# Decay attention into a softplus FFN on one core: three attention units loaded ahead of the weights, the weights' top bits shared between ScalarE and VectorE, and 12 instead of 10 units with whole float32 operands

## The chip, the cores and the metric

The kernel runs on one core of a Trainium2 chip. The metric is the device time of one execution in microseconds (us). Before the change it was 701.85 us, the median of three runs from 699.92 to 701.89.

## What is computed

A linear attention with a decay per head feeds a two-layer FFN with a softplus between the layers. Inputs q, k, v are float32 of shape (4, 8, 768, 64); the weights are float64 of shape (512, 2048) and (2048, 512).

```python
gamma = 1.0 - 2.0 ** (-5.0 - np.arange(H, dtype=np.float32))
for t in range(S):
    state = gamma[None, :, None, None] * state + np.einsum('bhd,bhe->bhde', k[:, :, t], v[:, :, t])
    y[:, :, t] = scale * np.einsum('bhd,bhde->bhe', q[:, :, t], state)
...
x = np.ascontiguousarray(attn_out.transpose(0, 2, 1, 3)).reshape(B * S, H * D)
h = x @ w_in
g = np.maximum(h, 0.0) + np.log1p(np.exp(-np.abs(h)))
return (g @ w_out).astype(np.float32)
```

## The kernel before

**Attention.** The sequence is cut into chunks of C = 128 tokens. A unit is one chunk of one batch entry for half of the heads (4 heads): 48 units, in the order batch, chunk, half. Within a unit the work is quadratic, and a state of 64 x 64 per head carries the decay over to the next chunk. A unit goes through these parts:

- `load_unit` (L104): three loads on SP's queue, kn, qn, vn, of 128 KB each, with three buffers of each.
- `decay` (L113): GpSimd multiplies qn and vn by the decay tables.
- `operands` (L120): TensorE transposes kn and qn into the PSUM tile tp; ScalarE and VectorE copy it out.
- `scores` (L156): TensorE makes sc = k q^T, ScalarE copies it to ah, GpSimd masks it (L177).
- `new_state` (L182): TensorE makes pp = k^T v; VectorE adds it to the running sum td. The last chunk of a sequence leaves this out.
- `stack_and_outputs` (L259): ScalarE copies the state to st; TensorE makes yp from st and qw and from vn and ah; ScalarE casts it to xh (L255), VectorE writes the remainder xl (L257).

Tiles tp, sc, pp and yp share three PSUM buffers.

**Precision.** A product of two float32 operands is made in one of two ways. For the first WHOLE = 10 units the operands stay float32 ("whole"): one matmul, which the trace shows as two rows. For later units each operand is split into a high part in float32r and a remainder, and a product is made of three float32r matmuls or of matmuls with the parts side by side (L139 to L153, L171, L195, L242 to L251). The split needs more copies and subtractions on ScalarE and VectorE.

**Weights.** The float64 weights are loaded as 16 slices f of both matrices (`load_weights`, L62; 512 KB each, on SP's queue) and converted in place of a cast (`convert_weights`, L74). For each slice of w_in and of w_out, words low and high are the two halves of a float64. ScalarE rescales the high word (L82) and takes the top three bits of the low word into wp by a multiplication with a rounding offset (L87). VectorE joins sign and bits (L88, L89) into the float32 w. ScalarE casts w to its float32r high part (L91), GpSimd subtracts for the remainder (L92). wp is one buffer in PSUM; w has two. The load of slice f waits for the casts of slice f - FETCH (3).

**FFN.** For blocks of T = 256 tokens and pairs of slices, `hidden` (L279) makes 24 matmuls into hp (L286 to L288), softplus runs over VectorE, ScalarE, VectorE, ScalarE, GpSimd (L293 to L302), and `second` (L305), two steps later, adds 12 matmuls into acc (L316 to L318).

**Order.** Parts of unit u are due at tick 4u plus an offset (`PARTS`, L264). A first loop (L371) runs the ticks up to those of block 0; in it, every fourth tick loads one slice of weights and, from the fourth slice on, converts one. Then the steps follow, with ticks planned between them. The program is then ordered on each engine by a scheduler with a timeline of its own, so that the order of a queue isn't that of the code: it is read from the compiled order. Each engine works its list in order.

Of the kernel before, what the change touches and what calls it, by code (L numbers as in the profile page):

```python
# [14 lines left out]
AF = mybir.ActivationFunctionType  # L15
ALU = mybir.AluOpType
# [3 lines left out]
T = 256  # L20
AHEAD = 2
EARLY = 2
WHOLE = 10
TURN = 5
LAG = 2
FETCH = 3
SLACK = 2.0**-17
# [3 lines left out]
def decay_attention_then_softplus_ffn(ctx: ExitStack, tc: tile.TileContext, q, k, v, w_in, w_out, qtab, vtab, gtab, out):  # L31
    nc = tc.nc
# [27 lines left out]
    raw, win, wout, converts = {}, {}, {}, {}  # L60

    def load_weights(f):  # L62
        fs = slice(f * P, (f + 1) * P)
        raw[f] = [const.tile([P, ND * P], I64, name=nm, tag=f"{nm}{f}") for nm in ("win", "wout")]
        loads_of_f = (
            nc.sync.dma_start(raw[f][0].rearrange("p (c w) -> p c w", c=ND), w_in[:, fs].rearrange("(c p) w -> p c w", p=P)),
            nc.sync.dma_start(raw[f][1], w_out[fs, :]),
        )

        if f >= FETCH:  # L70
            for load, after in zip(loads_of_f, converts[f - FETCH]):
                tc.add_manual_dep(load.ins, after.name, mybir.DependencyInfo(mybir.DependencyClass.Sync, mybir.DependencyReason.SCHED_ONLY), reason="pace")

    def convert_weights(f):  # L74

        n = ND * P
        converts[f] = []
        for nm, bits, to in zip(("win", "wout"), raw.pop(f), (win, wout)):
            words = bits.bitcast(U32).rearrange("p (n t) -> p n t", t=2)
            low, high = words[:, :, 0], words[:, :, 1]  # L80

            nc.scalar.activation(high.bitcast(F32), high.bitcast(F32), AF.Copy, scale=2.0**-112)  # L82

            wp = ps_w.tile([P, n], U32, name="wp")
            w = wts.tile([P, n], U32, name="w")

            nc.scalar.activation(wp, low, AF.Copy, scale=(1 - SLACK) * 2.0**-29, bias=7.5 * SLACK - 0.5)  # L87
            nc.vector.scalar_tensor_tensor(wp, high, 0x80000000, wp, op0=ALU.bitwise_and, op1=ALU.bitwise_or)  # L88
            nc.vector.scalar_tensor_tensor(w, high, 3, wp, op0=ALU.logical_shift_left, op1=ALU.bitwise_or)  # L89
            to[f] = const.tile([P, 2, n], F32R, name=f"{nm}hl", tag=f"{nm}{f}")  # L90
            converts[f].append(nc.scalar.copy(to[f][:, 0], w.bitcast(F32)).ins)  # L91
            nc.gpsimd.tensor_tensor(to[f][:, 1], w.bitcast(F32), to[f][:, 0].bitcast(F32), op=ALU.subtract)  # L92
# [3 lines left out]
    loads, live, state, xs = {}, {}, {}, {}  # L96
# [5 lines left out]
    qws = [attn.tile([P, 2, NJ, C], F32, name="qw", tag="vhl", bufs=2) for i in range(2)]  # L102

    def load_unit(n):  # L104
        b, c, hf = units[n]
        tiles = []
        for nm, src in (("kn", k), ("qn", q), ("vn", v)):
            t = attn.tile([P, HH, D], F32, name=nm, bufs=3)
            nc.sync.dma_start(t, src[b, hf * HH:(hf + 1) * HH, c * C:(c + 1) * C, :].rearrange("h s d -> s h d"))
            tiles.append(t)  # L110
        loads[n] = tiles
# [8 lines left out]
    def operands(n):  # L120
# [5 lines left out]
        for j in range(NJ):  # L126
            nc.tensor.transpose(tp[:, 1, j, :], qn[:, 2 * j:2 * j + 2, :], ident)  # L127
        if n < WHOLE:
            kw = attn.tile([P, NJ, C], F32, name="kw", tag="kh")
# [26 lines left out]
    def scores(n):  # L156
        kq = live[n][0]
        if n < WHOLE:
            kw, qw = kq
# [22 lines left out]
    def new_state(n):  # L182
# [4 lines left out]
        pp = ps_a.tile([D, HH, 2, D], F32, name="pp", tag="a")  # L187
        if n < WHOLE:
            kn, vn = live[n][1:3]
# [10 lines left out]
        else:  # L200
            td = state[hf][1]
            nc.vector.tensor_tensor(td, pp[:, :, 0, :], td, op=ALU.add)
        if n >= WHOLE:
            nc.vector.tensor_tensor(td, pp[:, :, 1, :], td, op=ALU.add)
        state[hf] = [None, td]

    def stack_state(n):
# [3 lines left out]
        tdv = state[hf][1].rearrange("d (j p) e -> d p j e", p=2)  # L211
        if n + 2 < WHOLE:
            st = attn.tile([P, NJ, D], F32, name=f"st{hf}", bufs=2)
# [13 lines left out]
    def outputs(n):  # L227
# [7 lines left out]
        for j in range(NJ):  # L235
            for par in range(2):
                h = 2 * j + par
                o = yp[:, par, j, :]
                if c and n < WHOLE:
                    nc.tensor.matmul(o, lhsT=st[:, j, :], rhs=kq[1][:, par, j, :], start=True, stop=False)  # L240
# [21 lines left out]


    PARTS = {-6: load_unit, -2: decay, 0: operands, 2: scores, 3: new_state, 5: stack_and_outputs}  # L264
    FIRST_TICK = min(PARTS)
    PERIOD = 4
# [3 lines left out]
    def tick(n):  # L270
        for at, part in PARTS.items():
            u, r = divmod(n - at, PERIOD)
            if r == 0 and 0 <= u < len(units):
                part(u)
# [64 lines left out]
    def ticks_for(i):  # L339

        return min(per_block * (i + 1) + max(PARTS) - PERIOD + 1 + AHEAD, last_tick + 1)

    done, loaded, converted = FIRST_TICK + 1, 0, 0

    def convert_to(n):
        nonlocal loaded, converted
        while converted < min(NF, n):
            convert_weights(converted)
            converted += 1
            if loaded < NF:  # L350
                load_weights(loaded)
                loaded += 1

    tick(FIRST_TICK)

    nc.scalar.dma_start(qtabs[:, 0], qtab)
    nc.scalar.dma_start(vtabs[:, 0], vtab)
# [13 lines left out]
    while done < ticks_for(0):  # L371
        tick(done)
        done += 1
        if done % 4 == 2:
            if loaded >= FETCH:
                convert_weights(converted)
                converted += 1
            load_weights(loaded)
            loaded += 1
# [66 lines left out]
```

## Time and profile before

| | |
|---|---|
| median of three runs | 701.85 us (699.92, 701.85, 701.89) |
| the profiled execution | 700.03 us |
| its span, first to last instruction | 698.2 us |
| ScalarE, VectorE, GpSimd busy | 372.1, 433.2, 281.4 us |
| DMA | 42.82 MB |

The profile is of one execution, whose own time is 700.03 us. PE is TensorE's matmuls, PEld its weight loads, DVE VectorE, ACT ScalarE, POOL GpSimd, SP the queue that issues the loads. L286 is line 286 of the kernel before. In a row of the timeline the first number is the start in us from the span's begin, the second the duration; a bracket names the idle time ahead and what ended it. In a row of a group stand the busy time of all, the mean of one in ns, and the idle time ahead. Starts of neighbouring matmuls are closer than their durations, since matmuls are pipelined: what one costs in a dense stretch is the distance of two starts.

### The profile page before, as it was taken

What the parts mean: (1) busy time and instruction counts of PE and PEld (TensorE: products, weight loads), DVE (VectorE), ACT (ScalarE), POOL (GpSimd) and SP (SyncE); (2) the same over time, 40 slices, a digit from 0 to 9 for tenths busy, and PEclk for the clock granted to TensorE, in tenths of its full rate; (3) what the DMA queues carried; (4) which work ended last, traced back from release to release, by engine and by line L of the source; (5) the groups of instructions that cost most, each with busy time, mean ns of one, the idle gap of its engine ahead of it and who ended that gap; (6) DMA issues with size and microseconds to landing.
All of it is one profiled execution on the core that took longest, in us unless ns stands there. A gap on an engine that the chain in (4) does not pass through costs nothing.

```text
span 698.2 us, 13537 instructions
## 1 busy us (share of the span) xinstructions
PE 684.4 (98%) x5056; PEld 621.3 (89%) x5056; DVE 433.2 (62%) x893; ACT 372.1 (53%) x835; POOL 281.4 (40%) x324
## 2 busy tenths in 40 slices
PE   6899999999999999999999999999999999999997
PEld 4688889899999999999999999999999999999996
DVE  4676785557666766557667666647766676544221
ACT  6988885446556546445555555445555544543221
POOL 5676667334343342343334333433433333222221
PEclk9999999999999999999999999999999999999999
DMA  9976650122112112111111111211211110000000
GB/s 266 287 201 173 192 159 1 31 61 69 31 23 69 31 25 61 31 31 54 39 23 37 49 38 24 61 37 25 62 24 39 54 31 16 31 1 1 31 1 30
DMA packets 90752, 42.82 MB, mean 61 GB/s; under 512 B 77376, under 2 KB 85568, under 8 KB 90688
## 3 DMA queue, kind: packets, MB, share of 16 engines
q1 hardware_dynamic: 90240, 41.96, 22.2%
q8 instruction: 40, 0.66, 0.4%
q14 instruction: 24, 0.20, 0.1%
q10 hardware_dynamic: 448, 0.01, 0.0%
HBM read 35.66 MB, written 6.29 MB: 60 GB/s over the span
## 4 chain that ended last, share of the span: by engine, by line
PE 96%; ACT 1%; issue 0%; DVE 0%; ACTq 0%
PE hp L286 14%; PE hp L287 13%; PE hp L288 13%; PE acc L316 13%; PE acc L317 13%; PE acc L318 13%; PE sc L171 3%; PE tp L125 1%; PE tp L127 1%; PE pp L195 1%; PE yp L250 1%; PE yp L251 1%; PE yp L249 1%; PE yp L246 1%; PE yp L240 1%; PE yp L243 1%
## 5 line engine op out<-in xcount | busy, mean ns | idle before, releaser
L286 PE MATMUL hp<-xh,winhl 128*128 128x256 f32 x768 | 221.4, 289 | 0.4 <-ACT xh L255 0.4
L288 PE MATMUL hp<-xh,winhl 128*128 128x256 f32 x768 | 217.9, 284 | 0.0
L287 PE MATMUL hp<-xl,winhl 128*128 128x256 f32 x768 | 217.6, 283 | 0.0
L302 POOL TENSOR_TENSOR gl<-sp,gh 128x512 fp32r<-128x512 f32 x96 | 125.4, 1306 | 149.3 <-ACT gh L300 86.7
L316 PE MATMUL acc<-wouthl,gh 128*128 128x512 f32 x384 | 154.3, 402 | 0.0
L317 PE MATMUL acc<-wouthl,gh 128*128 128x512 f32 x384 | 150.4, 392 | 0.0
L318 PE MATMUL acc<-wouthl,gl 128*128 128x512 f32 x384 | 149.1, 390 | 0.0
L286 PEld LDWEIGHTS hp<-xh,winhl 128*128 128x128 f32 x768 | 146.5, 191 | 2.8 <-issue 0.5
L287 PEld LDWEIGHTS hp<-xl,winhl 128*128 128x128 f32 x768 | 147.0, 191 | 1.6 <-issue 0.5
L288 PEld LDWEIGHTS hp<-xh,winhl 128*128 128x128 f32 x768 | 146.8, 191 | 0.6 <-issue 0.3
L293 DVE TENSOR_SCALAR sp<-hp 128x512 uint32<-128x512 uint32 x96 | 66.1, 690 | 70.6 <-PE hp L288 61.0
L300 ACT CAST gh<-sp 128x512 fp32r<-128x512 f32 x96 | 59.5, 620 | 74.1 <-PE acc L317 57.4
L117 POOL TENSOR_TENSOR qn<-qn,qtabs 128x256 f32<-128x256 f32 x48 | 29.4, 613 | 151.1 <-DMA qn<-in_q_dram 125.0
L294 ACT ACTIVATE sp<-sp 128x512 f32<-128x512 f32 x96 | 60.9, 634 | 49.0 <-DVE sp L293 48.7
L318 PEld LDWEIGHTS acc<-wouthl,gl 128*128 128x128 f32 x384 | 71.9, 188 | 15.6
L316 PEld LDWEIGHTS acc<-wouthl,gh 128*128 128x128 f32 x384 | 72.4, 189 | 12.5 <-issue 0.5
L317 PEld LDWEIGHTS acc<-wouthl,gh 128*128 128x128 f32 x384 | 72.5, 189 | 11.4
L298 DVE SCALAR_TENSOR_TENSOR sp<-hp,sp 128x512 f32<-128x512 f32 x96 | 65.9, 687 | 12.8 <-ACT sp L294 11.6
L142 DVE TENSOR_TENSOR kq<-tp,kq 64x256 fp32r<-64x256 f32 x76 | 32.1, 422 | 67.0 <-ACT kq L140 65.8
L139 ACT CAST kq<-tp 64x512 fp32r<-64x512 f32 x76 | 44.1, 581 | 40.0 <-PE tp L127 38.8
L255 ACT CAST xh<-yp 64x256 fp32r<-64x256 f32 x96 | 35.1, 366 | 51.0 <-PE yp L251 44.5
L257 DVE TENSOR_TENSOR xl<-yp,xh 64x256 fp32r<-64x256 f32 x96 | 39.9, 416 | 33.7 <-ACT xh L255 32.7
(85 smaller groups left out, 1082.6 us busy)
## 6 DMA issues: line engine op xcount, KB each, us to landing
win<-in_moe_w_in_dram SPq DMA_DIRECT2D x16, 512.0 KB, 4.5
wout<-in_moe_w_out_dram SPq DMA_DIRECT2D x16, 512.0 KB, 4.4
kn<-in_k_dram SPq DMA_DIRECT2D x48, 128.0 KB, 2.3
qn<-in_q_dram SPq DMA_DIRECT2D x48, 128.0 KB, 2.8
vn<-in_v_dram SPq DMA_DIRECT2D x48, 128.0 KB, 2.2
out_dram<-o SPq DMA_DIRECT2D x24, 256.0 KB, 2.1
gtab_sb<-in_gtab_dram ACTq DMA_DIRECT2D x2, 2.0 KB, 3.8
qtabs<-in_qtab_dram ACTq DMA_DIRECT2D x1, 4.0 KB, 2.4
```

The source lines that it names most:

```text
L139: nc.scalar.copy(kq[own, :2, par], tp[own])
L286: nc.tensor.matmul(hp[:, k], lhsT=wt[:, 0, d, :], rhs=xh[:, d, :], start=d == 0, stop=False)
L287: nc.tensor.matmul(hp[:, k], lhsT=wt[:, 0, d, :], rhs=xl[:, d, :], start=False, stop=False)
L288: nc.tensor.matmul(hp[:, k], lhsT=wt[:, 1, d, :], rhs=xh[:, d, :], start=False, stop=d == ND - 1)
L293: nc.vector.tensor_scalar(sp.bitcast(U32), hps[s].bitcast(U32), 0x80000000, None, op0=ALU.bitwise_or)
L294: nc.scalar.activation(sp, sp, AF.Softplus)
L298: nc.vector.scalar_tensor_tensor(g, hps.pop(s), 0.0, g, op0=ALU.max, op1=ALU.add)
L300: nc.scalar.copy(gh, g)
L302: nc.gpsimd.tensor_tensor(gl, sps.pop(s), gh.bitcast(F32), op=ALU.subtract)
L316: nc.tensor.matmul(acc[i][t], lhsT=gh[:, k, ts], rhs=wt[:, 0], start=begins and k == 0, stop=False)
L317: nc.tensor.matmul(acc[i][t], lhsT=gh[:, k, ts], rhs=wt[:, 1], start=False, stop=False)
L318: nc.tensor.matmul(acc[i][t], lhsT=gl[:, k, ts], rhs=wt[:, 0], start=False, stop=ends and k == 1)
```

## The change

Three edits.

1. Loads: units 0, 1 and 2 are loaded ahead of the first weights; `load_unit` returns at once for a unit that is loaded. The first loop starts one tick earlier; weights are loaded at its first tick and then at every fourth, one tick later than before, so that after it as many slices are loaded (6) and converted (3) as before.
2. Top bits: ScalarE takes them for w_out as before; for w_in VectorE shifts the low word right by 29 bits.
3. WHOLE is 12: units 10 and 11, the last chunk of batch entry 0, have whole float32 operands.

```diff
-WHOLE = 10
+WHOLE = 12
...
-            nc.scalar.activation(wp, low, AF.Copy, scale=(1 - SLACK) * 2.0**-29, bias=7.5 * SLACK - 0.5)
+            if nm == "wout":
+                nc.scalar.activation(wp, low, AF.Copy, scale=(1 - SLACK) * 2.0**-29, bias=7.5 * SLACK - 0.5)
+            else:
+                nc.vector.tensor_scalar(wp, low, 29, None, op0=ALU.logical_shift_right)
...
     def load_unit(n):
+        if n in loads:
+            return
...
-    done, loaded, converted = FIRST_TICK + 1, 0, 0
+    done, loaded, converted = FIRST_TICK, 0, 0
...
-    tick(FIRST_TICK)
+
+    for n in range(3):
+        load_unit(n)
...
-        if done % 4 == 2:
+        if done % 4 == 3 and done > 0 or done < 0 and loaded == 0:
```

Line numbers after are higher by 5 behind the edits: L82 stays, L87 is L88, L91 is L94, L131 is L136, L164 is L169, L255 is L260, L286 is L291.

On SP's queue the first 15 loads were kn, qn, vn and a slice of win and wout for units 0, 1 and 2 in turn; now the nine loads of the three units come first, then two slices of win and wout, then kn and qn of unit 3.

ScalarE's list from its first instruction on data, kw of unit 0, before (kw, qw: copies of the transposed operands; st: state; winhl, wouthl: the float32r weights):

```order
L131 COPY kw<-tp 128x256
L132 COPY qw<-tp 64x256
L82 ACTIVATE win<-win 128x512
L87 ACTIVATE wp<-win 128x512
L82 ACTIVATE wout<-wout 128x512
L214 COPY st_178<-td_167 64x128
L215 COPY st_178<-td_167 64x128
L164 COPY ah<-sc 128x512
L91 CAST winhl<-w 128x512
L87 ACTIVATE wp<-wout 128x512
L131 COPY kw<-tp 128x256
L132 COPY qw<-tp 64x256
```

The same place after:

```order
L136 COPY kw<-tp 128x256
L137 COPY qw<-tp 64x256
L219 COPY st_178<-td_167 64x128
L220 COPY st_178<-td_167 64x128
L169 COPY ah<-sc 128x512
L136 COPY kw<-tp 128x256
L137 COPY qw<-tp 64x256
L82 ACTIVATE win<-win 128x512
L260 CAST xh<-yp 64x2x128 x2
L82 ACTIVATE wout<-wout 128x512
L169 COPY ah<-sc 128x512
L94 CAST winhl<-w 128x512
```

The conversion of the first slice has moved behind unit 1's operands, and the first cast of weights behind unit 1's ah.

TensorE's list around the first hidden-layer matmul (hp), before; pp ahead of it is that of unit 3:

```order
L240 MATMUL yp<-qw,st_178 64x128
L246 MATMUL yp<-ah,vn 64x128
L191 MATMUL pp<-vn,kn 64x64 x4
L286 MATMUL hp<-xh,winhl 128x256 x2
L125 MATMUL tp<-ident,kn 128x128 x2
L127 MATMUL tp<-ident,qn 128x128 x2
L240 MATMUL yp<-qw,st_228 64x128
L287 MATMUL hp<-xl,winhl 128x256
```

And after:

```order
L245 MATMUL yp<-qw,st_178 64x128
L251 MATMUL yp<-ah,vn 64x128
L168 MATMUL sc<-qw,kw 128x128 x4
L291 MATMUL hp<-xh,winhl 128x256
L292 MATMUL hp<-xl,winhl 128x256
L293 MATMUL hp<-xh,winhl 128x256
L291 MATMUL hp<-xh,winhl 128x256
L292 MATMUL hp<-xl,winhl 128x256
L293 MATMUL hp<-xh,winhl 128x256
L196 MATMUL pp<-vn,kn 64x64 x4
L130 MATMUL tp<-ident,kn 128x128 x2
L132 MATMUL tp<-ident,qn 128x128 x2
```

Unit 3's sc has moved directly ahead of the first hp, and its pp behind the first six; these now include products with xl.

## The prediction

> **What bounds the kernel now.** I read the page first, then the busy time by windows, then the timeline of the first 34 us, and at last the groups by form for single prices. The page:
>
> ```profile
> span 698.2 us, 13537 instructions
> PE 684.4 (98%) x5056; PEld 621.3 (89%) x5056; DVE 433.2 (62%) x893; ACT 372.1 (53%) x835; POOL 281.4 (40%) x324
> PE 96%; ACT 1%; issue 0%; DVE 0%; ACTq 0%
> ```
>
> The third line is the chain that ended last: 96% of it is TensorE (PE). The windows tell where the rest lies (columns: length, busy us of PE, weight loads, VectorE, ScalarE, GpSimd, then clock, DMA share, GB/s):
>
> ```profile
> 0.00:10.00 10.00, 4.75 (x21) 3.65 (x22) 2.83 (x15) 4.25 (x8) 4.45 (x17) 1.00 0.84 225
> 10.00:20.00 10.00, 7.73 (x49) 5.62 (x47) 6.53 (x12) 8.89 (x21) 7.88 (x10) 1.00 1.16 316
> 20.00:30.00 10.00, 7.79 (x63) 6.21 (x62) 6.28 (x12) 8.96 (x21) 6.54 (x8) 1.00 1.10 296
> 30.00:40.00 10.00, 10.00 (x83) 8.86 (x82) 7.55 (x15) 9.15 (x21) 6.99 (x9) 1.00 0.79 222
> 80.00:90.00 10.00, 10.00 (x74) 8.81 (x74) 8.09 (x13) 8.80 (x18) 7.45 (x8) 1.00 0.59 167
> 90.00:100.00 10.00, 10.00 (x68) 8.97 (x67) 8.74 (x15) 8.24 (x16) 5.25 (x5) 1.00 0.47 131
> ```
>
> From 30 us on PE has no idle time. So the change can act in two ways only: it can start the dense stretch earlier, in the first 28 us, or it can change the amount of PE work behind that. In those 28 us the busy engine is ScalarE (8.89 and 8.96 of 10 us). The rows that mark the start (start us, duration, engine, line):
>
> ```profile
> 3.60 0.66 PE L125 MATMUL tp<-ident,kn 128*128 128x128 f32 x2 [3.60 <-DMA kn<-in_k_dram]
> 6.82 0.66 ACT L82 ACTIVATE win<-win 128x512 f32<-128x512 f32 x1 [0.28 <-DMA win<-in_moe_w_in_dram]
> 8.36 1.65 PE L163 MATMUL sc<-qw,kw 128*128 128x128 f32 x6
> 10.05 0.59 ACT L164 COPY ah<-sc 128x512 f32<-128x512 f32 x1 [0.26 <-PE sc L163]
> 11.40 1.64 PE L246 MATMUL yp<-ah,vn 128*64 128x128 f32 x8 [0.17 <-POOL ah L177]
> 26.90 0.74 ACT L255 CAST xh<-yp 64x256 fp32r<-64x256 f32 x2 [0.93 <-PE yp L246]
> 27.70 0.51 PE L286 MATMUL hp<-xh,winhl 128*128 128x256 f32 x2 [0.37 <-ACT xh L255]
> ```
>
> The first FFN matmul (27.70) waits for the xh cast of unit 2, which ScalarE reaches at 26.90. From there on hidden-layer matmuls fill every gap that attention leaves.
>
> **The change part by part: the start.** Prices of ScalarE's steps, means over the whole run:
>
> ```profile
> L82 ACT ACTIVATE win<-win 128x512 f32<-128x512 f32 x16 | 10.8, 678 | 2.1 <-DMA win<-in_moe_w_in_dram 2.1
> L82 ACT ACTIVATE wout<-wout 128x512 f32<-128x512 f32 x16 | 10.8, 676 | 1.5 <-DMA wout<-in_moe_w_out_dram 1.3
> L87 ACT ACTIVATE wp<-wout 128x512 uint32<-128x512 uint32 x16 | 10.1, 634 | 0.0
> L87 ACT ACTIVATE wp<-win 128x512 uint32<-128x512 uint32 x16 | 10.1, 631 | 0.0
> L91 ACT CAST wouthl<-w 128x512 fp32r<-128x512 f32 x16 | 9.9, 618 | 5.1 <-DVE w L89 5.0
> L91 ACT CAST winhl<-w 128x512 fp32r<-128x512 f32 x16 | 9.9, 616 | 1.0 <-DVE w L89 0.9
> L164 ACT COPY ah<-sc 128x512 f32<-128x512 f32 x10 | 5.8, 579 | 1.6 <-PE sc L163 1.4
> L131 ACT COPY kw<-tp 128x256 f32<-128x256 f32 x10 | 3.7, 366 | 3.8 <-PE tp L127 3.8
> L132 ACT COPY qw<-tp 64x256 f32<-64x256 f32 x10 | 3.6, 362 | 0.0
> L214 ACT COPY st<-td 64x128 f32<-64x128 f32 x8 | 2.3, 289 | 0.0
> L255 ACT CAST xh<-yp 64x256 fp32r<-64x256 f32 x96 | 35.1, 366 | 51.0 <-PE yp L251 44.5
> ```
>
> I count ScalarE's instructions in its order from the first ah copy (10.05 us) to the end of unit 2's xh pair. Before, they are 35: 3 ah, 3 pairs of kw and qw, 2 pairs of st, 3 pairs of xh, 6 of L82, 5 of L87 and 5 of L91. By the rows that is 3 x 0.58 + 3 x 0.73 + 2 x 0.58 + 3 x 0.73 + 6 x 0.68 + 5 x 0.63 + 5 x 0.62 = 17.6 us. The trace takes from 10.05 to 26.90 + 0.74 = 27.64, also 17.6 us: small waits and small overlaps cancel, so the sum is a fair clock.
>
> After, 30 instructions stand there. The 3 ah, the 3 kw/qw pairs, 2 st pairs and 3 xh pairs are the same; L82 is again 6, but the top bits on ScalarE are only 2 and the casts 3. Sum: 17.6 - 3 x 0.63 - 2 x 0.62 = 14.5 us, so 3.1 us less. Of this, the top bits of w_in are what moved to VectorE; the rest is conversions that stand later, since the weights are loaded later. The first ah can't come earlier: it waits for the six sc matmuls at 8.36, which end at 10.01, and PE's order up to there is the same.
>
> Part of the 3.1 us is lost. After the order goes ah, kw, qw, L82, and is through with these at 10.05 + 0.58 + 0.37 + 0.36 + 0.68 = 12.0. The next is unit 0's xh, which waits for the yp matmuls at 11.40 + 1.64 = 13.0. Before, other conversion steps filled that hole. So 1.0 us of waiting is new, and the first FFN matmul comes 2.1 us earlier, at about 25.6. It also has less behind it: PE's order before has unit 3's pp matmuls ahead of it, after they stand behind. Their cost is the distance of two starts, 33.68 - 33.07 = 0.6 us (rows below). What the start gains is 2.1 - 0.6 = **1.5 us**. Its ends: nothing, if ScalarE waits elsewhere as much as it saves, and 3.1 us, if the new wait and the pp cost vanish in other gaps.
>
> The three early units by themselves give little: of PE's waits in the rows above only the first, at 3.60, is for a load. The weights come later instead: six more loads of 0.13 MB stand ahead of them, 0.79 MB at 225 to 316 GB/s, about 2.9 us. The first L82 could then start at 6.82 + 2.9 = 9.7; ScalarE comes to it at 11.4. This costs nothing as long as that margin of 1.7 us holds; past it each us is paid in full by the casts behind. On SP's queue the loads of unit 3 now stand behind two sets of weights, before behind three. On GpSimd the decay of units 1 and 2 moves ahead of the first low parts of the weights, for which only the third matmul of each hidden group waits.
>
> **The half pace at the start.** The same matmuls are slow at first: six sc matmul rows take 1.65 us at 8.36, eight take 1.16 at 31.98, and pp falls from 1.12 us at 7.32 to the following:
>
> ```profile
> 7.32 1.12 PE L191 MATMUL pp<-vn,kn 128*64 128x64 f32 x8
> 14.52 0.68 PE L191 MATMUL pp<-vn,kn 128*64 128x64 f32 x8
> 30.31 0.43 PE L246 MATMUL yp<-ah,vn 128*64 128x128 f32 x2
> 31.98 1.16 PE L163 MATMUL sc<-qw,kw 128*128 128x128 f32 x8
> 33.07 0.68 PE L191 MATMUL pp<-vn,kn 128*64 128x64 f32 x8
> 33.68 0.51 PE L286 MATMUL hp<-xh,winhl 128*128 128x256 f32 x2
> ```
>
> The clock column of the windows says 1.00 all along, so it doesn't show this. I take it to end where it ended, between 11.4 and 14.5 us, since PE does the same work up to there; the sum above rests on that. The Trainium skill, "TensorE: Matmul & The Clock Gate", Part 1, has TensorE start at half clock, released by one busy window of about 3.4 us whose phase is free, and taken back by an idle one. The factor in these rows agrees with that. By that rule a start one window earlier is possible, and it would make the sum that of the faster rival below; an idle stretch of a whole window would make it worse, and my longest one is about 2 us.
>
> **Units 10 and 11 with whole operands.** This is PE work in the dense stretch and is paid in full. Rows of the split form, and two rows for the pitch of whole matmuls:
>
> ```profile
> 125.57 0.38 PE L240 MATMUL yp<-qw,st 128*64 128x128 f32 x2
> 125.79 0.38 PE L246 MATMUL yp<-ah,vn 128*64 128x128 f32 x2
> 129.51 0.64 PE L171 MATMUL sc<-kq 128*128 128x256 f32 x4
> 130.00 0.40 PE L316 MATMUL acc<-wouthl,gh 128*128 128x512 f32 x1
> 136.06 0.22 PE L242 MATMUL yp<-kq,st 128*64 128x128 f32 x1
> 137.26 0.33 PE L171 MATMUL sc<-kq 128*128 128x256 f32 x1
> ```
>
> Split: 4 sc matmuls take 130.00 - 129.51 = 0.49 us, 20 yp matmuls 137.26 - 136.06 = 1.20, together 1.69. Whole: one matmul (two rows) is 125.79 - 125.57 = 0.22, so 4 + 8 of them are 2.64, which is 0.95 more; for two units 1.9. Measured in place with the changes of shape around them, sc is 33.07 - 31.98 = 1.09 and seven yp matmuls 31.98 - 30.31 = 1.67, eight 1.91: 3.00, or 1.31 more, for two units 2.6. Both units are the last chunk of their sequence and have no pp. I take **2.1 us**, near the lower end, because PE's order after has fewer stretches of like matmuls in all (398 against 411 by my count), so the changes of shape that the two units add are saved elsewhere. What they save on ScalarE and VectorE lies beside a full PE and is worth nothing there.
>
> **Top bits of w_in on VectorE.** The nearest row is a one-source step of the same size:
>
> ```profile
> L293 DVE TENSOR_SCALAR sp<-hp 128x512 uint32<-128x512 uint32 x96 | 66.1, 690 | 70.6 <-PE hp L288 61.0
> ```
>
> 16 x 0.69 = 11.0 us more on VectorE, spread to about 105 us, and 16 x 0.63 = 10.1 us less on ScalarE. The tightest windows, 80 to 100, have 1.9 + 1.3 = 3.2 us of VectorE idle; about three of the 16 steps fall there, 2.1 us, and unit 10's splits leave. It fits: cost zero, hidden by PE; if it didn't fit, PE would wait one for one.
>
> **Sum.** The profiled execution took 700.03 us, 1.8 more than its span. 700.03 - 1.5 + 2.1 = 700.6. The three runs are 699.92, 701.85 and 701.89; the profile resembles the lowest, and the median is 1.8 higher. Put on the median the forecast is **702.4**, 0.6 above it. 0.3%, or 2.1 us, is about what a measurement of this kernel can tell from no change.
>
> **The rivals.**
>
> *The start runs at full pace (faster).* With units 1 and 2 there early, PE reaches full pace before the first sc. Then the six sc cost 0.9 instead of 1.65, pp 0.7 instead of 1.1, yp 0.95 instead of 1.64, and the new 1.0 us wait goes: 2.8 us more, with the 1.5 a gain of 4.3, so 701.85 - 4.3 + 2.1 = 699.6. For it: the slow rows. Against it: PE's early waits are for ScalarE and GpSimd, not for loads. Chance 0.2, with whatever else shortens the start.
>
> *VectorE's longer chain takes the place of the ScalarE step (slower).* ScalarE works in order; its cast of w_in waits for VectorE, which now runs three dependent steps for it, and xh and ah of the units queue behind that cast. If each of the three casts ahead of the first FFN matmul waits 0.69 us, 2.1 us are lost: 701.85 + 2.1 + 2.1 - 1.5 = 704.5. For it: the casts of wouthl waited 5.0 us for VectorE before. Against it: winhl only 0.9, and the shift needs the load alone, so it can run ahead. It decides once these waits exceed 1.5 us in sum. Chance 0.18.
>
> *The change doesn't do what it says (slower or same).* ScalarE's freed time goes into waiting, the start gains nothing, the whole units stay: 701.85 + 2.1 = 704.0, on the border of 0.3%. Chance 0.12, half to each side.
>
> **How the numbers follow.** The forecast has 0.50; its own range, with gain 0 to 3.1 and cost 1.9 to 2.6, is 700.6 to 704.5. Faster by over 0.3%: 0.20. Slower: 0.18 + 0.06 = 0.24. Within: 0.50 + 0.06 = 0.56. The range takes in the first two rivals, with 0.6 us for runs that fall low like the profile: 699.0 to 704.8.
>
> **What would show it.** Right: the first hp matmul at 25 to 26 us, PE at 10.00 in every window from 30 on, and PE busy after 30 us longer by about 2 us. Wrong on the start: first hp at 23 us or at 27 and later; waits of winhl's cast on VectorE well over 1 us before 28 us. Wrong on VectorE: a window between 80 and 110 us in which PE falls under 10.00. Wrong on the units: whole sc and yp of units 10 and 11 at other distances than 1.1 and 1.9 us.

## The result, and the profile after

The changed kernel takes 704.74 us (median of 6 runs, 703.70 to 705.78), the kernel before on the same chip 700.84 us (6 runs, 699.92 to 701.89). The ratio is 1.0053 with a 95% interval of 1.0038 to 1.0068: slower by 0.5%, 3.9 us. I had taken 702.4 and "no change" for the likeliest, with 704.8 as the upper end.

Runs of one kernel fall on two levels some 1.8 us apart, the upper one with the lower mean granted clock (before 699.9 to 700.1 and 701.6 to 701.9; after 703.7 to 703.9 at 0.998 and 705.6 to 705.8 at 0.994 to 0.995), so that a median can lie between them. The profiled executions, 700.03 and 703.89, are 3.86 us apart, and this difference can be followed in the trace.

The page of the changed kernel, the lines that answer to those of before (span, busy time of the engines, the chain that ended last):

```profile
span 702.1 us, 13473 instructions
PE 687.4 (98%) x5056; PEld 624.3 (89%) x5056; DVE 435.8 (62%) x889; ACT 360.5 (51%) x809; POOL 280.0 (40%) x322
PE 95%; ACT 1%; DMA 1%; issue 1%; DVE 1%; POOL 0%; SPq 0%; DVEq 0%; ACTq 0%; POOLq 0%
```

TensorE still carries the chain. The windows of the changed kernel (columns as before: PE, weight loads, VectorE, ScalarE, GpSimd, clock, DMA share, GB/s):

```profile
0.00:10.00 10.00, 4.65 (x21) 3.54 (x22) 2.08 (x13) 2.51 (x5) 6.07 (x19) 1.00 0.79 185
10.00:20.00 10.00, 8.01 (x63) 6.34 (x61) 7.05 (x14) 8.53 (x20) 3.86 (x6) 1.00 1.10 323
20.00:30.00 10.00, 8.22 (x65) 6.88 (x65) 7.16 (x14) 8.56 (x21) 8.45 (x11) 1.00 0.97 271
30.00:40.00 10.00, 10.00 (x82) 8.77 (x81) 8.59 (x16) 8.19 (x19) 6.34 (x9) 1.00 0.82 233
80.00:90.00 10.00, 8.30 (x51) 6.69 (x50) 6.97 (x12) 7.21 (x14) 4.87 (x6) 0.95 0.62 189
90.00:100.00 10.00, 10.00 (x62) 8.90 (x62) 7.25 (x13) 6.19 (x11) 6.93 (x7) 0.88 0.50 161
```

The start is better than before: 63 and 65 matmuls in the second and third window, before 49 and 63 (the numbers behind x in PE's column). But PE idles 1.7 us in 80 to 90, where it had no idle time, and from there to 100 us the granted clock is under 1. TensorE's timeline at that place (start, duration, engine, line, what, and idle time ahead with its releaser):

```profile
85.57 0.28 PE L293 MATMUL hp<-xh,winhl 128*128 128x256 f32 x1
85.69 0.39 PE L168 MATMUL sc<-qw,kw 128*128 128x128 f32 x2
86.81 0.44 PE L130 MATMUL tp<-ident,kn 128*128 128x128 f32 x2 [0.73 <-ACT ah L169]
87.08 0.38 PE L132 MATMUL tp<-ident,qn 128*128 128x128 f32 x2
88.43 0.39 PE L291 MATMUL hp<-xh,winhl 128*128 128x256 f32 x1 [0.97 <-DVE sp L303]
...
88.90 0.34 PE L291 MATMUL hp<-xh,winhl 128*128 128x256 f32 x1
...
89.25 0.42 PE L293 MATMUL hp<-xh,winhl 128*128 128x256 f32 x1
89.46 0.42 PE L291 MATMUL hp<-xh,winhl 128*128 128x256 f32 x1
...
92.43 0.28 PE L293 MATMUL hp<-xh,winhl 128*128 128x256 f32 x1
```

Two waits, 0.73 and 0.97 us, and then hp matmuls that start 0.21 us apart (89.25, 89.46) instead of 0.12. From 88.90 to 92.43 seventeen of them take 3.53 us; at 0.12 that would be 2.04, so 1.5 us are lost to half pace. The first wait is for ScalarE's copy of sc (86.17), the second for hp. Why PE waits at 88.43 is seen on VectorE and ScalarE. VectorE first:

```profile
85.89 1.29 DVE L298 TENSOR_SCALAR sp<-hp 128x512 uint32<-128x512 uint32 x2 [1.08 <-PE hp L293]
...
87.69 0.68 DVE L303 SCALAR_TENSOR_TENSOR sp<-hp,sp 128x512 f32<-128x512 f32 x1
```

ScalarE at the same time:

```profile
86.17 0.58 ACT L169 COPY ah<-sc 128x512 f32<-128x512 f32 x1 [0.68 <-PE sc L168]
86.65 1.25 ACT L299 ACTIVATE sp<-sp 128x512 f32<-128x512 f32 x2
```

The fifth and the sixth hidden step (the last of block 0's first five and the first of block 1) are interleaved on PE at this place and end together at 85.7 us, and both hp buffers are then full. The seventh step needs one of them back, which takes VectorE, ScalarE and VectorE again: from 85.69 to 88.37, 2.7 us. For that time PE must have other work in its list. In the changed kernel it has one sc matmul and four transposes there; in the kernel before 3 acc, 1 yp, 4 sc and 4 pp matmuls stood there, and PE didn't wait. From the last hp of the sixth step to the first of the seventh it is about as long in both, 2.97 us before (81.33 to 84.30) and 2.86 after (85.57 to 88.43); the one stretch is full of work, the other mostly empty. The softplus chain itself is as long before: from 81.45, behind the last hp row, to 83.46 + 0.68 = 84.14, also 2.7 us. Rows of the kernel before, PE and VectorE:

```profile
81.33 0.28 PE L288 MATMUL hp<-xh,winhl 128*128 128x256 f32 x1
83.46 0.68 DVE L298 SCALAR_TENSOR_TENSOR sp<-hp,sp 128x512 f32<-128x512 f32 x1
84.30 0.39 PE L286 MATMUL hp<-xh,winhl 128*128 128x256 f32 x1
```

To place the difference I counted each matmul at its pitch at full pace (0.12 us for hp, 0.23 for acc, 0.03 to 0.22 for the others, the usual distance of two starts) and took what PE needs beyond that ("loss"), by stage. In us, from the traces:

| kernel | pitch of all matmuls | loss to 36 | 36 to 80 | 80 to 100 | behind |
|---|---|---|---|---|---|
| before | 664.2 | 18.1 | 5.4 | 1.1 | 4.9 |
| after | 666.1 | 16.4 | 5.4 | 5.1 | 4.8 |

So the start gains 1.7 us, the two whole units add 1.9, and the hole with its half-paced stretch adds 4.0: together 4.1 at the last matmul; the spans differ by 3.9.

### The profile page after: what moved, and what is told of

Its sections match the earlier page's. It is cut to its first block, busy times and chain, and to the rows that moved or that the text cites. A ratio compares the mean times of both kernels' runs of the same rounds, so it can differ in the third digit from the quotient of the medians.

```text
span 702.1 us, 13473 instructions
## 1 busy us (share of the span) xinstructions
PE 687.4 (98%) x5056; PEld 624.3 (89%) x5056; DVE 435.8 (62%) x889; ACT 360.5 (51%) x809; POOL 280.0 (40%) x322
## 4 chain that ended last, share of the span: by engine, by line
PE 95%; ACT 1%; DMA 1%; issue 1%; DVE 1%; POOL 0%; SPq 0%; DVEq 0%; ACTq 0%; POOLq 0%
PE hp L291 14%; PE hp L292 13%; PE hp L293 13%; PE acc L321 13%; PE acc L322 13%; PE acc L323 13%; PE sc L176 2%; PE tp L130 1%; PE yp L251 1%; PE pp L200 1%; PE yp L245 1%; PE tp L132 1%; PE yp L256 1%; PE yp L255 1%; PE yp L254 1%; PE yp L248 1%
## 5 line engine op out<-in xcount | busy, mean ns | idle before, releaser
L291 PE MATMUL hp<-xh,winhl 128*128 128x256 f32 x768 | 222.7, 290 | 1.9 <-DVE sp L303 1.0
L291 PEld LDWEIGHTS hp<-xh,winhl 128*128 128x128 f32 x768 | 147.4, 192 | 4.7 <-DVE sp L303 1.2
L147 DVE TENSOR_TENSOR kq<-tp,kq 64x256 fp32r<-64x256 f32 x72 | 30.4, 422 | 62.8 <-ACT kq L145 61.7
L144 ACT CAST kq<-tp 64x512 fp32r<-64x512 f32 x72 | 41.9, 581 | 43.3 <-PE tp L132 42.4
L260 ACT CAST xh<-yp 64x256 fp32r<-64x256 f32 x96 | 35.0, 364 | 50.0 <-PE yp L256 45.2
```

Of the source, the lines that this page charges most:

```text
L144: nc.scalar.copy(kq[own, :2, par], tp[own])
L291: nc.tensor.matmul(hp[:, k], lhsT=wt[:, 0, d, :], rhs=xh[:, d, :], start=d == 0, stop=False)
```

## The experiments

"Sixth to seventh" is the number of matmuls that stand in PE's compiled list between the last hp matmul of the sixth hidden step and the first of the seventh. The waits are PE's waits at that place in the trace; half pace is what the granted clock shows behind 30 us. Ratios are against the kernel before on the same chip (701.42 us for the first four experiments, 700.14 for the next four, 701.25 for the last three). A matmul of whole operands counts once, though the trace has two rows of it. (The expectations say 11 for the kernel before and E7; by the trace it is 12.) The profiled executions of E1, E2 and E3 have one more half-paced stretch of 3.4 us at the start, from 26.72, 23.74 and 23.01 us, which is in their loss to 36 us.

| kernel | us | ratio (95%) | sixth to seventh | PE waits there, us | half pace | loss to 36 | 80 to 100 |
|---|---|---|---|---|---|---|---|
| before | 700.84 | | 12 | none | none | 18.1 | 1.1 |
| after | 704.74 | 1.0053 (1.0038 to 1.0068) | 5 | 0.73 + 0.97 | 3.4 us | 16.4 | 5.1 |
| E1 after, 10 whole | 704.13 | 1.0042 (1.0029 to 1.0054) | 6 | 2.62 | 3.4 us | 18.4 | 4.7 |
| E2 before, 12 whole | 702.67 | 1.0024 (1.0013 to 1.0034) | 12 | none | none | 19.5 | 0.8 |
| E3 before, bits alone | 699.26 | 0.9975 (0.9966 to 0.9985) | 17 | 0.21 + 0.60 | none | 18.8 | 2.4 |
| E4 loads alone | 705.53 | 1.0065 (1.0053 to 1.0078) | 4 | 3.69 | 6.8 us | 16.1 | 7.1 |
| E5 after, looser pacing | 704.76 | 1.0062 (1.0050 to 1.0074) | 15 | 1.22 | 3.4 us, at 35 us | 20.1 | 2.2 |
| E6 after, first weights first | 698.75 | 0.9975 (0.9965 to 0.9984) | 20 | 0.42 | none | 16.0 | 1.0 |
| E7 before, late weights | 704.76 | 1.0066 (1.0054 to 1.0078) | 12 | none | none | 22.4 | 1.7 |
| E8 after, filler | 703.14 | 1.0045 (1.0033 to 1.0058) | 13 | 0.73 | none | 16.2 | 2.4 |
| E9 units on ScalarE's queue | 714.05 | 1.0190 (1.0174 to 1.0205) | 22 | none | none | 27.5 | 1.3 |
| E10 E6 with 10 whole | 697.86 | 0.9956 (0.9942 to 0.9970) | 19 | 0.22 | none | 16.6 | 2.0 |
| E11 E6, bits on ScalarE | 700.42 | 0.9994 (0.9985 to 1.0002) | 7 | 0.78 | none | 16.2 | 2.0 |

### One part at a time: E1 to E4

Theory A is the hole, rival B the whole units. E1 is the changed kernel with `WHOLE = 10`, E2 the kernel before with `WHOLE = 12`. E3 puts the second edit alone into the kernel before, E4 undoes the second and the third in the changed kernel, which leaves the loads:

```diff
 E1                                E2
-WHOLE = 12                       -WHOLE = 10
+WHOLE = 10                       +WHOLE = 12
 E3, in the kernel before (E4 undoes it, and WHOLE is 10)
+            if nm == "wout":
                 nc.scalar.activation(wp, low, AF.Copy, ...)
+            else:
+                nc.vector.tensor_scalar(wp, low, 29, None, op0=ALU.logical_shift_right)
```

> The changed kernel with WHOLE = 10 again: loads ahead and top bits alone. Theory A: the changed kernel lost 1.7 us to two PE waits at 86 to 88 us and 1.9 us to a half clock behind them, because TensorE's list has only 0.65 us of work between the end of two hidden steps that end together and the third, which needs a buffer that softplus frees some 2.7 us later; this list has 0.9 us there (2 sc, 4 tp), so the hole and the half clock stay and only the 1.9 us of whole units go: about 702.0, mean clock under 1.000. Rival B: the whole units of the change cost 4 us in place (copies, shapes, order) and the start gained nothing: about 700, clock 1.000.

> The kernel before with WHOLE = 12 alone. A: TensorE's list has 2 acc, 2 yp, 3 sc, 4 pp (about 2 us) at that place, so no hole; the price is the 1.9 us of PE work: about 702.0 against 700.0 for its fast level, clock 1.000. B: about 704.

> The kernel before with the top bits of w_in on VectorE alone. A: the list has sc, 4 pp, 4 tp, 8 yp (2.9 us) at the place, no hole; ScalarE's list ahead of the first hidden matmul is about 3 x 0.63 us shorter: 698.5 to 700, clock 1.000. B (the shift on VectorE is what delays softplus and makes the hole): a PE wait between 80 and 110 us and about 702.

> Loads ahead alone: top bits on ScalarE, WHOLE = 10. A: the list has only 4 tp (0.45 us) at the place: a hole of about 2 us and a half clock, about 703, clock under 1.000. B: no hole, since VectorE has no shift to do: 699 to 700.

E2 (702.67) and E3 (699.26) came out as A had it, and B is out: the whole units cost about half of the 4 us that B asks for, and the bits on VectorE are a gain. The medians, 1.25 us over the kernel before and 2.16 under it, mix runs of different mean clock in unlike shares. Runs at 0.999 to 1.000 alone have 702.09 (E2) and 698.93 (E3) against 700.00, which is 2.1 us more and 1.1 less. E4 has no shift on VectorE and the longest wait, so the shift doesn't make the hole either. E1 and E4 missed A's numbers by over 2 us upwards: their waits are longer than those of the changed kernel, and E1's profiled execution loses another 2.0 us ahead of 36 us, with the stretch from 26.72. E1, TensorE:

```profile
87.78 0.40 PE L176 MATMUL sc<-kq 128*128 128x256 f32 x2
90.81 0.41 PE L130 MATMUL tp<-ident,kn 128*128 128x128 f32 x2 [2.62 <-issue]
```

E4, windows; PE waits 3.69 us up to 91.36, and the clock is at half from 89.68, inside that wait, to 96.51:

```profile
80.00:90.00 10.00, 7.03 (x46) 6.13 (x44) 6.05 (x12) 5.90 (x11) 6.33 (x7) 0.98 0.53 168
90.00:100.00 10.00, 8.64 (x44) 8.21 (x45) 7.99 (x15) 8.21 (x16) 6.29 (x6) 0.67 0.49 140
```

Both waits end at the transposes, 0.1 us after VectorE's last step on the sc buffer of the unit ahead, though the bracket says "issue". The hp buffers come back late as well: the softplus chain takes 3.5 us in E1 (87.78 to 91.30) and 4.4 in E4 (87.51 to 91.86), because steps of the weights and of the split stand between its own on VectorE and ScalarE. E4 also waits 2.92 us up to 77.38, for the copies of unit operands, and 0.64 up to 86.21, for the low part of a slice of w_in.

So the hole comes with the loads, not with the other two edits. But how? The six loads put the first weights back by 3.6 us (SP issues them at 5.98 instead of 2.39), and casts of w_in stay 3 to 7 us behind those of before up to 83 us. That is theory C: late weights make PE run dry. Theory D says that PE's own list makes it: with the edit the scheduler writes another order, and too little stands between the sixth and the seventh step.

### Late weights or PE's list: E5 to E8

```diff
 E5 (FETCH stays 3)
-        if f >= FETCH:
-            for load, after in zip(loads_of_f, converts[f - FETCH]):
+        if f >= 6:
+            for load, after in zip(loads_of_f, converts[f - 6]):
 E6
-    for n in range(3):
-        load_unit(n)
+    load_unit(0), load_weights(0), load_unit(1), load_unit(2)
+    loaded = 1
 E7, in the kernel before; spare lies in room that is used later
     tick(FIRST_TICK)
+    for n in range(6):
+        nc.sync.dma_start(spare[n // 2][:, n % 2], k[0, :HH, C:2 * C, :].rearrange("h s d -> s h d"))
 E8, both loops of transposes
-        for j in range(NJ):
+        for j in (3 if n == 11 else 1) * list(range(NJ)):
```

> Changed kernel, but the load of weight slice f waits for the casts of slice f-6 instead of f-3, so that a stream that started late may catch up. Theory C (late weights: the w_in casts run 3 to 5 us late up to 80 us, unit steps on ScalarE queue behind them, and PE runs dry at 85 to 93 us): casts of w_in come back to the times of before by the sixth slice, the hole and its half-paced 3.4 us go, time 700.5 to 702.0. Theory D (it is PE's own list: between the sixth and seventh hidden step of the block stand only 1 sc and 4 transposes in the changed kernel, 11 matmuls before, whatever the weights do): here 15 matmuls stand there, so the hole goes as well, 700.5 to 702.5. The casts' times and the place of any hole that is left tell more than the time.

> Changed kernel, but the first weight slice is loaded between unit 0 and units 1 and 2. Theory C: the first conversion steps can start at the times of before, the casts of w_in are at most 1 us behind those of before, no hole at 85 to 93 us, time 700.5 to 702.0. Theory D: 20 matmuls stand between the sixth and seventh hidden step, no hole either, 700.5 to 702.5; the casts may stay 3 to 5 us late.

> Kernel before with six loads of 0.13 MB that nothing reads put ahead of the first weight load; PE's list stays word for word that of before. Theory C: the weights alone being 3 us late makes the hole and the half pace between 75 and 95 us; time 703.0 to 705.0. Theory D: with the 11 matmuls of before still between the sixth and seventh step PE bridges the softplus chain; only the start can lose something, time 700.5 to 702.5, and PE stays at 10.00 in every window from 30 us on.

> Changed kernel with the four transposes of unit 11 done three times over (8 more, about 0.9 us of PE work of no use), which stand in the hole between the sixth and seventh hidden step. If idling sets off the half-paced 3.4 us, PE now idles only 0.7 to 0.9 us there, the half pace goes and the time falls by about 1.8 us in spite of the added work: 702.5 to 703.3. If the half pace has another cause, the added work lies in the hole and the time stays at 704 to 705, or grows to 705.6 if the hole is no longer there to take it.

**E7** was to tell C and D apart at the hole. Its casts of w_in are at first nearly as late as those of the changed kernel (13.5, 21.3, 29.0, 35.8 us; after 15.1, 22.5, 28.6, 35.6), PE's list is that of before, and PE goes through without a wait:

```profile
86.14 0.28 PE L288 MATMUL hp<-xh,winhl 128*128 128x256 f32 x1
86.27 0.40 PE L316 MATMUL acc<-wouthl,gh 128*128 128x512 f32 x1
...
87.05 0.43 PE L246 MATMUL yp<-ah,vn 128*64 128x128 f32 x2
87.42 1.16 PE L163 MATMUL sc<-qw,kw 128*128 128x128 f32 x8
88.50 0.68 PE L191 MATMUL pp<-vn,kn 128*64 128x64 f32 x8
89.11 0.39 PE L286 MATMUL hp<-xh,winhl 128*128 128x256 f32 x1
```

Its 12 matmuls last from 86.27 to 89.11, 2.84 us, just longer than the softplus chain of 2.7. That is as D has it, but it is weaker than it looks: PE too runs 4.8 us later than before (the sixth step ends at 86.14 instead of 81.33, the eleventh cast starts at 84.7 instead of 79.9), so beside PE's work the weights aren't late. What speaks against C in the changed kernel are its own rows and E8: the softplus chain is no longer than before, the seventh step works on the third and fourth slice of w_in, whose casts start at 28.6 and 35.6 us, and the second wait goes with filler alone (below). So D holds for the hole of the changed kernel; in E1 and E4 the other steps on VectorE and ScalarE lengthen it. D's number for the time is wrong all the same: 704.76 instead of 700.5 to 702.5, with 4.3 us of loss more than before ahead of 36 us. In E7 units 1 and 2 come late as well, PE starves at the start, and it stays at half clock until 25.52 us. E7, TensorE at the start:

```profile
13.25 0.66 PE L125 MATMUL tp<-ident,kn 128*128 128x128 f32 x2 [3.12 <-DMA kn<-in_k_dram]
...
22.16 1.97 PE L246 MATMUL yp<-ah,vn 128*64 128x128 f32 x8 [0.58 <-POOL ah L177]
```

Eight yp rows take 1.97 us at half pace; the changed kernel has them in 1.09 us at 11.51.

**E6** moves one slice of weights ahead of units 1 and 2. The start is as good as that of the changed kernel (loss 16.0), PE's list comes out with 20 matmuls between the two steps, and the hole is gone. E6, TensorE:

```profile
78.91 1.06 PE L168 MATMUL sc<-qw,kw 128*128 128x128 f32 x8
79.89 0.68 PE L196 MATMUL pp<-vn,kn 128*64 128x64 f32 x8
80.99 0.44 PE L130 MATMUL tp<-ident,kn 128*128 128x128 f32 x2 [0.42 <-ACT ah L169]
```

698.75 us is 0.8% under the changed kernel by the two ratios, and faster than the kernel before. Both theories had asked for 700.5 or more; the 1.2 us less between 36 and 80 us were in neither.

**E8** adds 0.9 us of useless transposes in the hole, with casts of w_in as late as those of the changed kernel (71.1 and 77.6 us for the ninth and tenth, after 71.4 and 77.4). By the medians the time falls by 1.6 us, by the two ratios, whose intervals overlap, by 0.6. The profiled execution, the fastest of the six, takes 702.25 us. E8, TensorE:

```profile
86.58 0.88 PE L130 MATMUL tp<-ident,kn 128*128 128x128 f32 x6 [0.73 <-ACT ah L169]
87.29 0.82 PE L132 MATMUL tp<-ident,qn 128*128 128x128 f32 x6
88.20 0.39 PE L291 MATMUL hp<-xh,winhl 128*128 128x256 f32 x1
```

The second wait is filled, the hp matmuls behind it are 0.12 us apart (the next starts are 88.43, 88.55, 88.66), and the loss in 80 to 100 us is 2.7 less: 0.97 of the wait and about 1.5 of half pace make up 2.5 of it. Five of the six runs have a mean clock of 0.999 to 1.000, where all six of the changed kernel have 0.998 or less. So here idling sets off the half pace, and work of no use that prevents it costs no more than it saves.

**E5** was to let the late stream catch up, and failed. The loads run ahead, but the casts of w_in stay where they were (71.6 and 78.0 us for the ninth and tenth, after 71.4 and 77.4): the loads' pace doesn't set them; that ScalarE's list does is my reading and not tested. With 15 matmuls PE no longer waits for hp; it waits 1.22 us for td, the running sum of the state, and no half pace follows. A new one comes at 35 us in the profiled execution. The time, 704.76, is outside both theories' ranges, and the half pace at 35 us isn't the whole of it: two of the five runs have a mean clock of 1.000 and still take 703.8. E5, TensorE:

```profile
34.10 0.50 PE L291 MATMUL hp<-xh,winhl 128*128 128x256 f32 x2 [1.57 <-ACT xh L260]
...
88.45 0.43 PE L245 MATMUL yp<-qw,st 128*64 128x128 f32 x2 [1.22 <-DVE td L207]
```

### Prices on other lists: E9 to E11

```diff
 E9, in the changed kernel
-            nc.sync.dma_start(t, src[b, ...
+            (nc.scalar if n in (1, 2) else nc.sync).dma_start(t, src[b, ...
 E10, in E6
-WHOLE = 12
+WHOLE = 10
 E11, in E6: top bits of win and wout by the same activation on ScalarE
```

> Changed kernel with the loads of units 1 and 2 issued on ScalarE's DMA queue, so that the first weights follow unit 0 at once on SP's. Between the sixth and seventh hidden step PE's list has 22 matmuls (12 acc, 4 tp, 6 yp). Theory D (PE's list decides): no wait over 0.6 us between 75 and 95 us, no half pace after 30 us, 698.0 to 700.5. Theory C (lateness of the weights alone): the same, if the weights come early. A rival for the start: the six issues hold up ScalarE's first copies, and the start loses 1 to 2 us: 700 to 702.

> The kernel with the first weight slice ahead of units 1 and 2, with 10 units of whole operands instead of 12. If the two whole units cost what PE's work says (my 2.1 us, ends 1.9 and 2.6): 698.75 less 1.9 to 2.6 = 696.1 to 696.9, unless the list that comes out has a hole: between the sixth and seventh step stand 19 matmuls, between the seventh and eighth none. If whole units pay nothing, as the earlier pair on the changed kernel (704.1 against 704.7) could be read: 698 to 699.5.

> The kernel with the first weight slice ahead of units 1 and 2, with the top bits of w_in back on ScalarE. Theory D: between the sixth and seventh step only 7 matmuls are left in PE's list (3 yp, 4 sc, about 1.5 us), so a wait of about 1 us comes back there; together with ScalarE's longer list at the start (2 us in the pair of before with and without this part) 700.5 to 704. Theory C: the weights are early, so no hole: 698.5 to 701.

**E9** has no hole, as D said, but costs 13 us at the start, which no expectation had. ScalarE issues the six loads and, behind them, those of the decay tables, and reaches its first step on data at 13.19 us. GpSimd has the remainder of that weight slice ahead of unit 0's decay in its list, so the decay waits, and PE with it. E9, ScalarE, GpSimd and TensorE:

```profile
13.19 0.65 ACT L82 ACTIVATE win<-win 128x512 f32<-128x512 f32 x1 [11.10 <-issue]
16.15 1.28 POOL L95 TENSOR_TENSOR winhl<-w,winhl 128x512 fp32r<-128x512 f32 x1 [12.07 <-ACT winhl L94]
17.39 1.18 POOL L122 TENSOR_TENSOR qn<-qn,qtabs 128x256 f32<-128x256 f32 x2
18.06 0.69 PE L132 MATMUL tp<-ident,qn 128*128 128x128 f32 x2 [13.38 <-POOL qn L122]
```

**E10** is the fastest, 697.86 us, 0.4% under the kernel before. Against E6 it puts the price of the two whole units at 0.9 us (1.3 by the ratios), between the two cases that I had named; the runs of E10 and E6 overlap (696.6 to 699.3 and 698.4 to 699.7). By pitch the units are 1.9. But E10's list is another one, and it loses 0.6 us more than E6 ahead of 36 us and 1.0 more in 80 to 100, so the pair doesn't measure the units alone.

**E11** shows the bits again: 1.7 us (1.3 by the ratios) slower than E6 with them on ScalarE, the wait below included. With 7 matmuls in the list the wait is back, shorter than the 1 us that D had said:

```profile
84.16 1.16 PE L165 MATMUL sc<-qw,kw 128*128 128x128 f32 x8
86.10 0.36 PE L288 MATMUL hp<-xh,winhl 128*128 128x256 f32 x1 [0.78 <-DVE sp L300]
```

Its 700.42 us lies in C's range, and 0.1 us under D's; the wait for hp is D's. It doesn't settle the matter, since by then its casts are as late as in the changed kernel (70.3 and 76.7 us for the ninth and tenth). Over the thirteen kernels 4 to 7 matmuls left waits of 0.8 to 3.7 us, 12 and more waits of 0 to 1.2 us.

## Why the prediction missed its middle

The time lies inside the range, at its upper end, and slower than the likeliest case. That it is inside is luck: a gain of 1.7 at the start and 1.9 of added work are close to my own 1.5 and 2.1, and the 4.0 us on top come from a place that no term, end or rival of mine had.

- **The start: right in sum.** I took a gain of 1.5 us; the loss to 36 us is 1.7 less. Its parts shifted. The first hp matmul came at 24.33 us, 3.4 earlier than before and not 2.1, and half of that is lost again up to 36 us, where I had 0.6. The rival of full pace was half true: yp runs at full pace at once, while sc ahead of it is still slow. By the granted clock the half pace ended at 10.47 us, 2.1 earlier than before (12.56); in E1, with the same loads, it ended at 13.06, so this part can't be credited to the loads alone. Two rows of the changed kernel:

```profile
8.47 1.65 PE L168 MATMUL sc<-qw,kw 128*128 128x128 f32 x6
...
11.51 1.09 PE L251 MATMUL yp<-ah,vn 128*64 128x128 f32 x8 [0.72 <-POOL ah L182]
```

- **The whole units: right.** I took 2.1 us; PE's work grows by 1.9, and E2, where they are the only change, measures 2.1 at equal mean clock (1.7 by the ratio).
- **The bits on VectorE: right in sign.** I put the 16 shifts at zero, hidden by PE, and no run shows a price. The casts of winhl do wait longer for VectorE, 4.1 us in all instead of 0.9, but ahead of 28 us only once, for 0.53:

```profile
L90 DVE TENSOR_SCALAR wp<-win 128x512 uint32<-128x512 uint32 x16 | 11.1, 691 | 0.4
...
L94 ACT CAST winhl<-w 128x512 fp32r<-128x512 f32 x16 | 9.9, 617 | 4.3 <-DVE w L92 4.1
```

  And E3 and E11 make the edit a gain of 1.1 to 1.8 us. The rival in which this chain costs 2.1 us is refuted, although its time, 704.5, was close: a rival can hit the number and miss the cause. So can a sign: the one that I had named for VectorE, a window between 80 and 110 us with PE under 10.00, came, but it came in E4 too, which has no shift there.
- **Weights later at no cost: right at the start.** The loss to 36 us is 16.4 with the weights late and 16.0 with the first slice early (E6).
- **PE full from 30 us on: this step failed.** I wrote that from the first hp matmul on "hidden-layer matmuls fill every gap that attention leaves" and let the 1.5 and the 2.1 us add up on that. I read it off the trace of before, where it is so because 12 matmuls bridge a softplus chain of 2.7 us with 0.16 us to spare. The change rewrites PE's list as a whole, and I compared the two lists only in the first 28 us. At the next place where both hp buffers are full, the new list has five matmuls. No rival of mine had that, and the price is 4.0 us: 1.7 of waits, 1.5 of half pace, and 0.8 that I haven't placed.
- **Half pace: half right.** I assumed that it ends at the start as before (it ended earlier, see above) and doesn't come back, since my longest idle stretch was 2 us. It came back behind two waits of 1.7 us in sum.

Why the scheduler writes so short a list for the changed kernel is open: its own timeline decides it, and I only saw what it wrote.

## What to carry to other kernels

Where a scheduler writes the engines' lists, an edit at the start changes the order everywhere. Compare the compiled lists wherever both buffers of a long chain are full, and set the pitch of the matmuls that stand there beside the time in which the chain gives one buffer back. When a hidden engine is said to be free, ask how thin the cover is: here it was 2.84 us of matmuls over 2.7.

## What the runs showed of the hardware

Idling of well under 3.4 us can cost a half-paced stretch: in the changed kernel waits of 0.73 and 0.97 us that end 1.6 us apart, in E5's profiled execution one of 1.57 us, in each case followed by 3.4 us of half clock, in the changed kernel 1.5 us lost. Single waits of 1.22 (E5) and 0.78 us (E11) were not followed by it, and neither was E4's of 2.92 us up to 77.38: there the clock falls only at 89.68. So the length of a wait doesn't decide by itself. Where it lies may: in all thirteen traces the changes of the granted clock lie whole multiples of 3.41 us apart (10.47, 88.97 and 92.39 in the changed kernel). On that grid the changed kernel's two waits, 1.70 us, lie in one stretch, and E4's is split at 76.03 into 1.56 and 1.36. No clean threshold comes out of it: 1.38 us of idling in one stretch is followed by half clock in E3, at 23.01, and E4's 1.56 is not. The Trainium skill, "TensorE: Matmul & The Clock Gate", Part 1, gives half clock after one idle window of about 3.4 us or more. The length of the half-paced stretches agrees, the idle time that sets them off doesn't: here the measurement decides.

Six loads ahead of a transfer put its issue back by 3.6 us, 0.6 us each; the issues themselves take 0.37 to 0.51 us on SP's queue, and the rest are gaps between them. I had estimated 2.9 us, from the rate of the transfers. SP's queue in the changed kernel:

```profile
2.39 0.51 SPq L114 DMA_DIRECT2D kn<-in_k_dram  x1
3.36 0.37 SPq L114 DMA_DIRECT2D qn<-in_q_dram  x1
...
5.98 0.51 SPq L66 DMA_DIRECT2D win<-in_moe_w_in_dram  x1
```
